# v of pair 0 through the casting queue first, and the attention steps of batch 1 moved: what it does to a fused attention and MoE kernel

## The chip, the cores and the metric

One core of one Trainium2 chip. The metric is the device time of one execution in microseconds (us), median of several. The time before is 287.01 us (three runs, 286.96 to 287.21). The profile's span, from the first to the last instruction, is some 2 us shorter than that time.

## The reference, cut to what matters

```python
def _attn_ref(q, k, v, g_norm):            # q, k, v: 8 batches, 8 heads, 576 rows, 64 columns, float32
    kv = np.einsum('bhsd,bhse->bhde', k, v)
    out = np.einsum('bhsd,bhde->bhse', q, kv)
    rms = np.sqrt(np.mean(out * out, axis=-1, keepdims=True) + 1e-06)
    return out / rms * g_norm

def _moe_ref(x, w_in, w_out):              # x: 4608 x 512, w_in: 512 x 2048, w_out: 2048 x 512
    h = x @ w_in
    g = h * (1.0 / (1.0 + np.exp(-1.702 * h)))
    return g @ w_out
```

The attention's result, reordered to 4608 rows of 512, is the x of the second part. Inputs and output are float32.

Of the kernel before, what the change touches and what calls it, by code (L numbers as in the profile page):

```python
# [12 lines left out]
P = 128  # L13
# [3 lines left out]
def kernel(  # L17
# [10 lines left out]
    nc = tc.nc  # L28
# [6 lines left out]
    KO = DM // P  # L35
# [8 lines left out]
    PE_ = 96  # L44
# [29 lines left out]
    vbuf = const.tile([P, NPAIR, 2 * NJ * D], F16)  # L74
# [5 lines left out]
    w_in_sb = const.tile([P, KO, DFF], F16)  # L80
# [6 lines left out]
    def early_src(n, b, c0, c1):  # L87
        return srcs[n][b, 2 * c0 : 2 * c1].rearrange("h (p j) d -> p h (j d)", j=NJ)

    def early_load(n, b, c0, c1):  # L90
        nc.gpsimd.dma_start(  # L91
            out=raw[n][0:PE_, c0:c1, :].rearrange("p c (l x) -> p (c l) x", l=2),
            in_=early_src(n, b, c0, c1),
        )
# [45 lines left out]


    first = {}
    for n in "kqv":
        first[n] = stage.tile([P, H, J * D], F32, name=f"{n}f", tag=f"{n}f")
        first[n] = first[n].rearrange("p h x -> p (h x)")[0:PE_, 0 : 2 * NJ * D]
        dst, src = first[n].rearrange("p (h x) -> p h x", h=2), early_src(n, 0, 0, 1)
        nc.sync.dma_start(out=dst, in_=src)
    g_row = const.tile([1, D], F32)
    nc.scalar.dma_start(out=g_row, in_=g_norm.unsqueeze(0))
    nc.vector.memset(ident, 0.0)  # L150
    nc.vector.memset(kvb[1], 0.0)
    nc.gpsimd.affine_select(
        out=ident,
        in_=ident,
# [6 lines left out]
    nc.gpsimd.memset(ones2, 0.0)  # L161
    nc.gpsimd.memset(ones2[0:D, 0:D], 1.0)
    nc.gpsimd.memset(ones2[D:P, D:P], 1.0)

    def load_w_in(f0, f1, k0=0, k1=KO):
        nc.gpsimd.dma_start(
            out=w_in_sb[:, k0:k1, f0 * P : f1 * P],
            in_=moe_w_in[k0 * P : k1 * P, f0 * P : f1 * P].rearrange(
                "(ko ki) f -> ki ko f", ki=P
            ),  # L170
        )

    for c in range(1, NPAIR):
        for n in "qkv":
            early_load(n, 0, c, c + 1)
    load_w_in(0, 4, 0, 2)
    load_w_in(0, 4, 2, KO)
    load_w_in(4, GROUP)
    load_w_in(GROUP, 10)
    load_w_in(10, FO)  # L180
# [264 lines left out]
    def dense(t, units1, units2, group, deep, hid=None):  # L445
# [21 lines left out]
        def project(mo, fo):  # L467
# [10 lines left out]
            if fo == FO - 1:  # L478
# [3 lines left out]
                if t == B:  # L482
                    store_rest(mo, 0, DM)
                elif t in HALVED and mo % 2:
                    store(t, mo - 1, mo + 1)

        def store_rest(mo, n0, n1):
            for g in range(2):
                rows = out[(2 * mo + g) * S : (2 * mo + g + 1) * S, n0:n1]
                if 2 * mo + g < EARLY:  # L490
                    p0 = SM % PE_
                    rows = rows[bass.DynSlice(NJ * p0 + SM // PE_, R, step=NJ), :]
                else:
                    rows = rows[SM:S, :]
                queue = (nc.sync, nc.scalar)[g]
                queue.dma_start(out=rows, in_=osb[g * R : (g + 1) * R, mo, n0:n1])
# [29 lines left out]
        if t < EARLY:  # L526

            n = 0
            while n < SM:
# [6 lines left out]
                n += m  # L536
        elif t < B and t not in HALVED:
            store(t, 0, J)

    def store(t, j0, j1):  # L540
        nc.sync.dma_start(
            out=out[t * S : t * S + SM, :].rearrange("(p j) m -> p j m", j=J)[:, j0:j1],
            in_=osbs[t][:, j0:j1],
        )
# [3 lines left out]

    nc.scalar.copy(qraw[0:PE_, 0, :], first["q"])
    nc.vector.tensor_copy(kraw[0:PE_, 0, :], first["k"])  # L550
    nc.vector.tensor_copy(vbuf[0:PE_, 0, :], first["v"])


    idle_ps = ps_h.tile([P, SM], F32, name="idle", tag="hT")
# [73 lines left out]
    nc.gpsimd.dma_start(out=g_all, in_=g_norm.unsqueeze(0).to_broadcast([P, D]))  # L628

    osbs = {}  # L630
    HALVED = (2, 3, 4, 5, 6)
    live = {0: a0}

    def start(b):
# [2 lines left out]
    for t in range(NT):  # L637
        b = t + 1
        u1, u2 = {}, {}

        def at1(i, f, *args):
            u1.setdefault(i, []).append(lambda: f(*args))

        def at2(i, f, *args):
            u2.setdefault(i, []).append(lambda: f(*args))

        def of(b, name, *args):
            return lambda: getattr(live[b], name)(*args)

        if t == 0:  # L650
            at1(7, of(0, "out", NPAIR))
            at2(4, setattr, a0, "ss_pool", Attention.ss_pool)
            at2(4, of(0, "ss", NPAIR, True))
            at2(4, of(0, "apply", NPAIR))
            at1(8, start, 1)
            for l in range(2):
                r = slice(l * PH, (l + 1) * PH)
                at1(8, nc.vector.memset, kpad[r, :, :, (1 - l) * D : (2 - l) * D], 0.0)
            for c in range(NPAIR):
                at1(12, of(1, "pack_q", c))  # L660
                at2(9 + 3 * c, of(1, "q", c))
                at2((21, 21, 33, 33)[c], of(1, "pack_k", c))
                at2((25, 27, 42, 43)[c], of(1, "kv", c))
                o = (31, 34, 50, 53)[c]
                at2(o, of(1, "out", c))
                if c == NPAIR - 1:
                    at2(46, load_kv, 2)
                at2((38, 46, 56, 59)[c], of(1, "ss", c))
                at2((38, 46, 56, 59)[c], of(1, "apply", c))
        elif b < B:  # L670
            if t == 1:
                at2(46, setattr, live[1], "ss_pool", Attention.ss_pool)
                at2(46, of(1, "out", NPAIR))
                at2(53, of(1, "ss", NPAIR))
                at2(53, of(1, "apply", NPAIR))
            f0 = 5 if t == 1 else 2
            at1(f0, cast_q, b)
            at1(f0, start, b)
            at1(f0, of(b, "transpose_q"))
            if t + 2 < B:  # L680
                at1(f0, load_q, t + 2)
                at1((10 if t == 1 else 9) + 4, load_kv, t + 2)
            for c in range(NPAIR):
                at1(f0, of(b, "pack_k", c))
                at1((10 if t == 1 else 9) + c, of(b, "kv", c))
            at2(6, nc.scalar.preload_act_table_set, "natural_log_exp_and_others")
            for j in range(J):
                at2((1, 4, 8, 11)[j], of(b, "rows", j))
            at2(7, of(b, "turn", 0))
            at2(16, of(b, "turn", 2))  # L690
            at2(27, of(b, "out", NPAIR))
            at2(36, of(b, "ss", NPAIR))
            at2(36, of(b, "apply", NPAIR))
        dense(t, u1, u2, (GROUP, 5)[t] if t < 2 else 0, t == 0, None if t else d0)
# [30 lines left out]
```

## The kernel before: the parts that the change touches

The kernel works batch by batch. While TensorE does the dense layers of batch t, the attention of batch t+1 is slipped in between. Only batch 0 has nothing to hide behind: its q, k and v, four pairs of heads, must be loaded first. Filler matmuls (`busy`) are there to keep TensorE's clock up meanwhile.

There are two ways in. The SP queue loads float32, and VectorE or ScalarE casts afterwards. The queue of GpSimd casts to 16 bits on the way; this text calls it **the casting queue**. One load of one tensor of one pair reads 295 kB and, when cast, writes 147 kB (the profile calls that 144 KB).

```python
    def early_load(n, b, c0, c1):                       # the casting queue
        nc.gpsimd.dma_start(out=raw[n][0:PE_, c0:c1, :]..., in_=early_src(n, b, c0, c1))
    # [cut]
    for n in "kqv":                                     # pair 0: float32, SP queue
        # [cut: the stage tile]
        nc.sync.dma_start(out=dst, in_=src)
    # [cut: g_row on the ACT queue, two memsets on VectorE]
    nc.gpsimd.affine_select(out=ident, ...)
    nc.gpsimd.memset(ones2, 0.0)                        # and two more
    for c in range(1, NPAIR):                           # pairs 1 to 3: nine casting loads
        for n in "qkv":
            early_load(n, 0, c, c + 1)
    load_w_in(0, 4, 0, 2)                               # five loads of w_in behind them
    # [cut: four more]

    nc.scalar.copy(qraw[0:PE_, 0, :], first["q"])       # the casts of pair 0
    nc.vector.tensor_copy(kraw[0:PE_, 0, :], first["k"])
    nc.vector.tensor_copy(vbuf[0:PE_, 0, :], first["v"])

    busy(12)
    a0.q(0)                                             # transposes of q
    busy(2)
    a0.kv(0)                                            # k^T v of pair 0
    # [cut: busy(2), out(0), q(1), kv(1), sums(0), out(1)]
    a0.q(2)
    a0.rs(0)
    busy(1)
    a0.kv(2)
    # [cut: sums(1), apply(0), busy(1), out(2), rs(1)]
    a0.q(3)
    a0.kv(3)
    # [cut: sums(2), apply(1), out(3), rs(2), apply(2), busy(3), then the dense matmuls of batch 0]

    # batch 1, between the matmuls of batch 0's second dense layer (the numbers are places there)
                at2((25, 27, 42, 43)[c], of(1, "kv", c))
                o = (31, 34, 50, 53)[c]
                at2(o, of(1, "out", c))
```

## Time and profile before

| what | before | from |
|---|---|---|
| time, median | 287.01 us | timed runs |
| span of the profiled execution | 284.9 us | the page |
| TensorE busy | 279.1 us, 98% | the page, busy shares |
| kv of pair 3 starts | 12.90 us | timeline |
| first dense matmul | 14.55 us | timeline |

The busy shares of the page (engine, busy us, share of the span, instructions) and its DMA queues (q0 is the casting queue, q1 the SP queue; packets, MB written, share of 16 engines):

```profile
PE 279.1 (98%) x1717; PEld 135.1 (47%) x1717; DVE 118.9 (42%) x230; ACT 156.1 (55%) x273; POOL 57.1 (20%) x82
...
q0 software_dynamic: 14960, 15.58, 33.5%
q1 hardware_dynamic: 38688, 22.39, 30.2%
```

The reader is to see that TensorE is the bound for the whole and that DMA isn't, on average. An average hides the opening, where TensorE waits for loads; the prediction below takes it apart.

### The profile page before, as it was taken

Reading aid. Unit: us, or ns where it says so; the run is one execution under the profiler, and the core shown is the slowest. Engines: PE = TensorE matmul, PEld = TensorE weight load, DVE = VectorE, ACT = ScalarE, POOL = GpSimd, SP = SyncE. Lnnn points to the kernel's source line nnn. Section 1 sums busy time; section 2 is a strip of 40 time slices with the busy share of each in tenths; the row PEclk is TensorE's granted clock in tenths of the full one; section 3 lists DMA queues with packets and bytes.
Section 4 is the critical chain, followed back from the end, with each engine's and each line's share of the span. In section 5 each row is a group of like instructions: output and inputs, shape, how many; then the busy total and the mean of one; then the engine's idle time right before and its main releaser. Section 6 shows DMA issues by size and latency. Waiting matters only on the chain.

```text
span 284.9 us, 4354 instructions
## 1 busy us (share of the span) xinstructions
PE 279.1 (98%) x1717; PEld 135.1 (47%) x1717; DVE 118.9 (42%) x230; ACT 156.1 (55%) x273; POOL 57.1 (20%) x82
## 2 busy tenths in 40 slices
PE   8899999999999999999999999999999999999995
PEld 2444544455445544554455445544454444444443
DVE  2550666527661657157713852286327400110001
ACT  2697439766575646574458536763666365016400
POOL 8931461111211121112011401130002100000000
PEclk9999999999999999999999999999999999999999
DMA  8999999995589358953797279925401410012022
GB/s 176 200 207 204 205 249 239 242 268 105 122 165 254 60 147 161 242 90 69 224 208 138 38 216 200 184 39 184 83 2 37 120 66 0 0 69 81 0 74 74
DMA packets 54070, 38.76 MB, mean 136 GB/s; under 512 B 31219, under 2 KB 50931, under 8 KB 53923
## 3 DMA queue, kind: packets, MB, share of 16 engines
q0 software_dynamic: 14960, 15.58, 33.5%
q1 hardware_dynamic: 38688, 22.39, 30.2%
q10 hardware_dynamic: 402, 0.52, 0.5%
q8 instruction: 13, 0.21, 0.3%
q14 instruction: 7, 0.05, 0.1%
HBM read 36.73 MB, written 9.44 MB: 162 GB/s over the span
## 4 chain that ended last, share of the span: by engine, by line
PE 93%; POOL 2%; DMA 2%; DVE 1%; issue 0%
PE hT L434 44%; PE o L471 42%; PE kvp L223 3%; DMA vbuf<-in_v_dram 2%; PE outR L287 2%; PE oh L503 1%; POOL kraw L91 1%; PE ss L335 1%; POOL qraw L91 1%; DVE kpad L214 1%; PE outT L255 0%; POOL vbuf L91 0%; PE q L412 0%; PE outT L266 0%; PE idle L558 0%
## 5 line engine op out<-in xcount | busy, mean ns | idle before, releaser
L471 PE MATMUL o<-w_out_sb,gT 128*128 128x512 f16 x560 | 130.7, 379 | 0.0
L443 ACT ACTIVATE gT<-hT 128x512 f16<-128x512 f32 x144 | 84.5, 599 | 76.5 <-PE hT L434 76.4
L434 PE MATMUL hT<-xT,w_in_sb 128*128 128x512 f16 x512 | 116.2, 379 | 0.0
L434 PEld LDWEIGHTS <-w_in_sb 128*128 128x128 f16 x576 | 54.6, 98 | 62.3 <-DMA w_in_sb<-in_moe_w_in_dram 0.5
L471 PEld LDWEIGHTS <-gT 128*128 128x128 f16 x560 | 52.9, 98 | 56.2 <-issue 0.2
L481 DVE COPY osb<-o 128x512 f32<-128x512 f32 x20 | 13.8, 690 | 62.4 <-PE o L471 62.4
L319 POOL TENSOR_TENSOR x<-xr,g_all 128x512 f16<-128x512 f32 x12 | 15.2, 1270 | 71.2 <-DVE xr L312 47.2
L214 DVE COPY kpad<-kraw 64x576 f16<-64x576 f16 x56 | 25.0, 446 | 2.0 <-DMA kraw<-in_k_dram 0.7
L298 DVE TENSOR_REDUCE sum<-sq 128x8 f32<-128x512 f16 x24 | 15.8, 679 | 19.9 <-ACT sq L295 19.9
L236 DVE CAST kvb<-kvp 64x128 f16<-64x128 f32 x28 | 8.1, 288 | 36.5 <-PE kvp L223 36.4
L312 DVE TENSOR_TENSOR xr<-outR,sum 128x512 f32<-128x512 f32 x24 | 15.5, 686 | 11.1 <-ACT sum L309 11.1
L112 POOL DMA_DIRECT2D kraw<-in_k_dram x16 | 9.9, 624 | 48.8 <-DVE kpad L214 42.8
L112 POOL DMA_DIRECT2D vbuf<-in_v_dram x16 | 9.7, 608 | 33.9 <-PE kvp L223 29.3
L319 DVE TENSOR_TENSOR x<-xr,g_all 128x512 f16<-128x512 f32 x12 | 15.2, 1267 | 0.7
L295 ACT ACTIVATE sq<-outR 128x512 f16<-128x512 f32 x24 | 13.6, 591 | 2.0 <-PE outR L287 1.6
L223 PEld LDWEIGHTS <-kpad 128*128 128x128 f16 x252 | 11.0, 98 | 7.0 <-DVE kpad L214 0.9
L434 PE MATMUL hT<-x_rem,w_in_sb 128*128 128x512 f16 x64 | 14.0, 379 | 0.0
L275 ACT ACTIVATE sq<-outT 128x512 f16<-128x512 f32 (+1 forms) x16 | 7.7, 481 | 10.4 <-PE outT L255 9.0
L481 ACT COPY osb<-o 128x512 f32<-128x512 f32 x15 | 8.7, 581 | 6.3 <-DMA out_dram<-osb 6.3
L223 PE MATMUL kvp<-vbuf,kpad 128*128 128x64 f16 x252 | 11.9, 193 | 0.1
L308 ACT ACTIVATE sum<-sum,eps_t 128x16 f32<-128x16 f32 x12 | 3.7, 308 | 15.0 <-DVE sum L298 14.9
L337 ACT ACTIVATE ln<-ss,eps_t 128x512 f32<-128x512 f32 (+1 forms) x16 | 9.4, 586 | 4.3 <-PE ss L335 4.1
(62 smaller groups left out, 141.5 us busy)
## 6 DMA issues: line engine op xcount, KB each, us to landing
qf<-in_q_dram SPq DMA_DIRECT2D x5, 1024.0 KB, 9.0
out_dram<-osb SPq DMA_DIRECT2D x10, 512.0 KB, 2.9
kraw<-in_k_dram POOLq DMA_DIRECT2D x12, 288.0 KB, 6.9
vbuf<-in_v_dram POOLq DMA_DIRECT2D x12, 288.0 KB, 5.5
w_out_sb<-in_moe_w_out_dram POOLq DMA_DIRECT2D x3, 512.0 KB, 14.4
out_dram<-osb SPq DMA_DIRECT2D x6, 192.0 KB, 5.5
qf<-in_q_dram POOLq DMA_DIRECT2D x1, 1024.0 KB, 11.1
out_dram<-osb SPq DMA_DIRECT2D x1, 1024.0 KB, 3.8
```

The lines of the kernel that those rows point to most:

```text
L112: nc.gpsimd.dma_start(out=raw[n][l * PH : (l + 1) * PH, c0:c1, 0 : NH * D], in_=srcs[n][b].rearrange("(c l) (p j) d -> l p c (j d)", l=2, ...
L214: nc.vector.tensor_copy(out=kpad[r, c, :, l * D : (l + 1) * D], in_=kraw[r, c, 0 : NH * D].rearrange("p (j d) -> p j d", j=NH),)
L223: nc.tensor.matmul(self.kvp[:, c, :], kpad[:, c, j, :], vbuf[:, c, j * D : (j + 1) * D], start=(j == 0), stop=(j == NH - 1),)
L295: nc.scalar.activation(sq, t, AFT.Square)
L298: nc.vector.tensor_reduce(out=self.sum2[:, j % 2, :], in_=sq.rearrange("p (h d) -> p h d", h=H), op=ALU.add, axis=mybir.AxisListType.X,)
L312: nc.vector.tensor_mul(xr[:, i], self.o[j + i].rearrange("p (h d) -> p h d", h=H), s2[:, i, :].unsqueeze(2).to_broadcast([P, H, D]),)
L319: (nc.vector if i else nc.gpsimd).tensor_mul(self.x16[:, j + i, :].rearrange("p (h d) -> p h d", h=H), xr[:, i], g_all.unsqueeze(1).to_bro ...
L337: nc.scalar.activation(ln[:, 0:n], t[:, 0:n], AFT.Ln, bias=eps_t, scale=1.0 / D)
L434: nc.tensor.matmul(self.h[fo], w_in_sb[:, ko, fo * P : (fo + 1) * P], self.x[:, ko], start=(ko == 0), stop=(ko == KO - 1),)
L443: nc.scalar.activation(self.gT[:, fo, :], self.h[fo], AFT.Gelu_apprx_sigmoid)
L471: nc.tensor.matmul(os[mo], gT[:, fo, mo * P : (mo + 1) * P], w_out_sb[:, fo, :], start=(fo == 0), stop=(fo == FO - 1),)
L481: copy(osb[:, mo, :], os[mo])
```

## The change

The intent: v of pair 0 isn't needed before kv of pair 0, so it can take the casting queue, and if it is the first load there, that queue starts before ident and ones are made instead of after. k and q then have the SP queue to themselves, and VectorE loses a cast. The moved steps of batch 1 fit the later or earlier arrival of its loads, and tile 7 is stored in two halves.

```diff
     first = {}
-    for n in "kqv":
+    early_load("v", 0, 0, 1)
+    for n in "kq":
 [cut]
+    early_load("q", 0, 1, 2)
     nc.gpsimd.affine_select(
 [cut: ones2; load_w_in only moves up in the text]
     for c in range(1, NPAIR):
-        for n in "qkv":
+        for n in "qkv"[c == 1 :]:
             early_load(n, 0, c, c + 1)
 [cut]
-    nc.vector.tensor_copy(vbuf[0:PE_, 0, :], first["v"])
 [cut]
-    HALVED = (2, 3, 4, 5, 6)
+    HALVED = (2, 3, 4, 5, 6, 7)
 [cut]
-                at2((25, 27, 42, 43)[c], of(1, "kv", c))
-                o = (31, 34, 50, 53)[c]
+                at2((27, 28, 42, 43)[c], of(1, "kv", c))
+                o = (32, 35, 50, 53)[c]
```

More of the change, by code (lines that the diff above doesn't have):

```diff
@@ L151, with load_w_in @@
     nc.vector.memset(kvb[1], 0.0)
+    def load_w_in(f0, f1, k0=0, k1=KO):
+        nc.gpsimd.dma_start(
+            out=w_in_sb[:, k0:k1, f0 * P : f1 * P],
+            in_=moe_w_in[k0 * P : k1 * P, f0 * P : f1 * P].rearrange(
+                "(ko ki) f -> ki ko f", ki=P
+            ),
+        )
+    early_load("q", 0, 1, 2)
     nc.gpsimd.affine_select(
@@ L163 @@
     nc.gpsimd.memset(ones2[D:P, D:P], 1.0)
-    def load_w_in(f0, f1, k0=0, k1=KO):
-        nc.gpsimd.dma_start(
-            out=w_in_sb[:, k0:k1, f0 * P : f1 * P],
-            in_=moe_w_in[k0 * P : k1 * P, f0 * P : f1 * P].rearrange(
-                "(ko ki) f -> ki ko f", ki=P
-            ),
-        )
     for c in range(1, NPAIR):
-        for n in "qkv":
+        for n in "qkv"[c == 1 :]:
             early_load(n, 0, c, c + 1)
```

## The prediction

> **What bounds the kernel now.** I first read the busy shares of the page, then busy time by stretch, the waits, the chain and the timeline of the opening, and last the DMA view in short windows. The page gives TensorE 279.1 us busy of a span of 284.9. The busy time by stretch (columns: stretch, PE, PEld, DVE, ACT, POOL, granted clock, DMA share, GB/s) says where the missing 5.8 us lie:
>
> ```profile
> 0.00:1.27 1.27, 0.00 (x0) 0.00 (x0) 0.39 (x4) 0.00 (x0) 0.46 (x6) 1.00 0.00 0
> 1.27:14.55 13.28, 12.30 (x128) 5.55 (x129) 5.48 (x13) 7.01 (x11) 12.46 (x21) 1.00 1.16 207
> 14.55:46.00 31.45, 31.36 (x200) 15.04 (x199) 13.58 (x28) 20.59 (x35) 12.14 (x19) 1.00 1.22 220
> 46.00:226.00 180.00, 180.00 (x1120) 88.60 (x1119) 94.27 (x177) 108.36 (x195) 32.05 (x38) 1.00 0.68 147
> 281.50:284.90 3.40, 0.00 (x0) 0.00 (x0) 0.29 (x1) 0.00 (x0) 0.00 (x0) 1.00 0.29 77
> ```
>
> From 46 us to the last matmul TensorE has no hole, at full clock: nothing outside it can shorten that. Of the rest, 1.27 us is start-up, 3.40 the last copy and store. Only 13.28 - 12.30 = 0.98 us in the opening and 31.45 - 31.36 = 0.09 up to 46 us are waits. So the change can win **1.07 us at most**, 0.4% of 287.01, unless it removes matmuls, and the two matmul streams have the same number of them.
>
> What the 0.98 us waits for, from the timeline of the opening (start, length, engine, line, operation; in brackets the idle time and what ended it):
>
> ```profile
> 1.79 0.82 POOL L91 DMA_DIRECT2D qraw<-in_q_dram  x1
> 5.28 0.83 ACT L549 CAST qraw<-qf 96x768 f16<-96x768 f32 x1 [2.69 <-DMA qf<-in_q_dram]
> 6.16 0.45 PE L389 MATMUL q<-ident,qraw 96*64 96x96 f16 x12
> 6.55 0.56 DVE L551 CAST vbuf<-vf 96x768 f16<-96x768 f32 x1 [1.68 <-DMA vf<-in_v_dram]
> 12.90 0.38 PE L372 MATMUL kv<-vbuf,kraw 96*64 96x64 f16 x12 [0.70 <-DMA vbuf<-in_v_dram]
> 16.51 4.86 PEld L434 LDWEIGHTS <-w_in_sb 128*128 128x128 f16 x24 [0.35 <-DMA w_in_sb<-in_moe_w_in_dram]
> 23.41 4.98 PEld L434 LDWEIGHTS <-w_in_sb 128*128 128x128 f16 x24 [0.20 <-DMA w_in_sb<-in_moe_w_in_dram]
> ```
>
> The one large hole is 0.70 us before kv of pair 3, whose v is the ninth and last attention load of GpSimd's queue. The last two lines matter as much: the weight loads that come behind it in that queue land just when TensorE wants them (0.35 and 0.20 us of weight-load wait, no matmul hole). TensorE and the casting queue run **neck and neck**. TensorE can't keep a gain bigger than the queue's own advance by more than a tenth or two.
>
> The chain of waits tells how that queue works:
>
> ```profile
> 1.85 0.77 POOL qraw L91
> 6.35 0.88 POOL kraw L91
> 7.23 5.54 DMA vbuf<-in_v_dram
> 12.90 0.40 PE kv L372 x12
> ```
>
> The last load is issued at 7.23 and lands 5.54 us later, a backlog. In the DMA view by window, packets of this queue first come at about 5.0 us, 3.2 after the first issue, and then run without a break at some 200 GB/s of written bytes. For 5.7 to 12.7 us (queue, packets, MB, share of engines) it reads:
>
> ```profile
> q0 software_dynamic: 1913, 1.40, 130.2%
> q1 hardware_dynamic: 3, 0.00, 0.2%
> ```
>
> 1.40 MB in 7.0 us is 0.2 MB per us, so a load of 144 KB (147 kB) costs 0.74 us. Nine from 5.0 end at 11.7, and a landing comes about 1 us after the last packet: 12.7, as seen (12.77). The SP queue's three float32 loads fill the engines from 1.8 to about 5.4 us.
>
> **What the Trainium skill says.** "DMA: Bandwidth & Descriptors", section "Issuing engines are not separate DMA queues": transfers of all issuing engines run on the same 16 DMA engines and interleave. The trace agrees: between 5.1 and 5.4 us the two queues moved 36 packets each. So v of pair 0 doesn't become free by changing queue. The same page, section "SWDGE vs HWDGE vs iDMA", says that a cast in flight is for GpSimd's descriptors alone, hence the queue; its "Latency and other measured facts" puts the first byte at 0.6 us from SP and about 1 us from GpSimd. Here SP's packets come 1.1 us after issue; GpSimd's took 3.2 us in the opening, and in the steady part (issue at 82.64, first packets after 83.8, full rate from about 85.0) 1.2 and 2.4 us. For full rate I use the measured 2.4 to 3.2.
>
> **The change part by part.**
> (1) v of pair 0 leaves the SP queue: 295 kB of float32 that shared engines with k and q go, and the 0.56 us cast on VectorE goes with them. Nothing waited for that cast: TensorE was doing filler matmuls until 7.16. Gain on the path: 0.
> (2) It becomes the first load on GpSimd, ahead of the ident and ones work, with q of pair 1 next. SP's first issue is at 0.75, so I put this one there: 1.79 - 0.75 = 1.04 us earlier. The queue carries ten attention loads instead of nine, +0.74. Net advance 1.04 - 0.74 = **0.30 us** for everything behind, if the engines are free and the queue doesn't run dry.
> (3) It may run dry once. The two early issues take 0.82 + 0.63, then ident and ones take 1.85 - 1.02 = 0.83, so k of pair 1 is issued near 3.03 instead of 2.61. With 2.4 to 3.2 us to full rate it flows from 5.4 to 6.2; before, it flowed from 5.0 + 0.74 + sharing, near 6.0. So the advance from there lies between +0.5 and -0.2.
> (4) k and q of pair 0 now meet v's packets from 3.2 to 4.0 us on. q's landing was 5.2 us, its cast ended 6.11, and TensorE took it at 6.16, right as the 12 fillers ended. Any delay of q shifts the opening; some 70 to 200 kB shared by halves makes it an estimated 0.2 to 0.5 us. It eats into the 0.70 us hole, not the end time at once: the hole leaves 0.2 to 0.5 us to win.
> (5) The kv steps of batch 1 move from 25 and 27 to 27 and 28, out from 31 and 34 to 32 and 35. These are the same matmuls in another order; the weight-load wait on kpad is 0.9 us in two times, but the matmul hole in all of that stretch is 0.09. Gain 0 to 0.09.
> (6) The store of tile 7 in two halves: it is issued near 254 us, the DMA share there is 0.13, and the end is the store after 281.5. Gain 0.
>
> Sum: the smaller of the hole left (0.2 to 0.5) and the queue's advance (centre 0.2, plus 0.1 of slack), plus up to 0.09. I take 0.3 us: 287.01 - 0.3 = **286.7**.
>
> **The rivals.**
> A: q is late by much more. If v and q of pair 1 reach full rate by 2.5 us, half the traffic is theirs while q waits; q lands 1 us later, q(0) starts near 7.2, and as its 6.05 us of serial work to the end of q(3) keep their length, kv of pair 3 comes at 13.2 instead of 12.9. Time 287.3. Against it: the slow ramp of GpSimd's queue.
> B: the queue runs dry and the weights land later. The w_in waits at 16.5 and 23.4 become matmul holes of about 0.2 us, time 287.2. For it: GpSimd's 0.63 us per issue is close to the 0.74 us per load.
> C: the full gain. Mixed traffic is denser (the SP queue alone fell to 259 packets in 3.3 to 4.8 us, 173 per us, while both together later made 240), so the engines finish the whole earlier, the 0.70 hole closes, the weights follow: 287.01 - 0.8 = 286.2.
> D: all hidden: 287.0.
>
> **Range and chances.** The ceiling of 1.07 us bounds it above, the rivals put it from 286.2 to 287.3, and the three runs of before spread by 0.25. A difference over 2% would need 5.7 us, which no part can bring: 0.005 each way.
>
> **What would show it.** Right: the stretch from 46 us on unchanged in busy time; v of pair 0 issued at about 0.75 us and k of pair 1 near 3.0; q's cast on ScalarE starting 5.4 to 5.8; the hole before kv of pair 3 under 0.5 us; the first dense matmul 0.2 to 0.5 us before 14.55; kpad weight-load waits shorter. Wrong: a filler-to-q(0) hole over 0.8 us (A), larger w_in waits (B), no hole at kv of pair 3 and the dense part over 0.6 us earlier (C). It would be wrong altogether if TensorE's clock or the tail changed.

## The result and the profile after

The changed kernel took **288.04 us** in the median of six runs, 287.34 to 289.51; the kernel before, run between them, 287.00 (286.87 to 287.51). The ratio is 1.0039, with a 95% interval of 1.0014 to 1.0063. A ratio here is the mean time of one kernel's fast runs over that of the other's fast runs of the same rounds, so it isn't quite the ratio of the medians quoted. The change costs some 1.1 us (0.0039 times 287), where 0.3 us of gain were forecast, and the time scatters over 2.2 us instead of 0.6.

The profiled execution was the fastest of the six (span 285.6). Its busy time by stretch, in the columns of before:

```profile
1.27:14.55 13.28, 10.96 (x126) 4.99 (x127) 4.49 (x12) 6.38 (x10) 12.75 (x22) 1.00 1.14 180
14.55:46.00 31.45, 31.39 (x200) 15.18 (x199) 13.94 (x29) 20.61 (x36) 12.52 (x20) 1.00 1.22 221
46.00:226.00 180.00, 180.00 (x1120) 88.43 (x1118) 94.32 (x177) 108.91 (x196) 32.08 (x38) 1.00 0.68 146
...
282.20:285.60 3.40, 0.00 (x0) 0.00 (x0) 0.28 (x1) 0.00 (x0) 0.00 (x0) 1.00 0.29 77
```

From 46 us on nothing changed, and the tail is 3.40 us again. The opening is where the time went: 10.96 us of matmuls instead of 12.30, and the DMA moved 180 GB/s instead of 207. (Not all of the missing matmul time is waiting: TensorE's clock came up to full at 4.2 us in this execution and at 5.7 in that of before, so the same fillers took 4.20 us instead of 4.92.)

The timeline of the opening, with the lines that answer to those shown of before:

```profile
1.31 0.82 POOL L91 DMA_DIRECT2D vbuf<-in_v_dram  x1 [0.86 <-POOLq L709]
2.13 0.64 POOL L91 DMA_DIRECT2D qraw<-in_q_dram  x1
...
3.64 0.65 POOL L91 DMA_DIRECT2D kraw<-in_k_dram  x1
...
5.24 0.83 ACT L550 CAST qraw<-qf 96x768 f16<-96x768 f32 x1 [2.66 <-DMA qf<-in_q_dram]
...
11.27 0.38 PE L373 MATMUL kv<-vbuf,kraw 96*64 96x64 f16 x12 [0.68 <-DMA vbuf<-in_v_dram]
...
13.53 0.38 PE L373 MATMUL kv<-vbuf,kraw 96*64 96x64 f16 x12 [0.72 <-DMA vbuf<-in_v_dram]
...
15.38 0.33 PEld L435 LDWEIGHTS <-w_in_sb 128*128 128x128 f16 x3 [0.55 <-DMA w_in_sb<-in_moe_w_in_dram]
```

q's cast on ScalarE starts at 5.24 us, as before (5.28): k and q were not delayed. But v of pair 0 was issued at 1.31 us, not at 0.75; k of pair 1 at 3.64 (before: 2.61); there are two holes for loads now, before kv of pair 2 and of pair 3; and kv of pair 3 starts 13.53 - 12.90 = 0.63 us later. The span is 285.57 - 284.93 = 0.64 us longer. That one number, **the start of kv of pair 3**, turned out to carry the end: in sixteen of the twenty traces the span ends 272.0 to 272.4 us after it, whatever was done to the loads (the four others, e2, r2, e6 and e9, are told below). In thirteen of the twenty, the two compared here among them, TensorE waits there for v of pair 3, the last of the attention's loads. In the seven others (e5, e6, e8, e9, e11, e12, r2) no wait stands before it, and an earlier late load, more fillers or a lower clock has set it.

Next, how fast the casting queue ran. For each of two kernels, the DMA view from 5 to 11 us, the line of the casting queue; before:

```profile
q0 software_dynamic: 1597, 1.14, 124.5%
```

and after:

```profile
q0 software_dynamic: 1505, 1.07, 124.3%
```

The queue of before began at 5.05 us and moved more in these 6 us than that of after, which had been running since 3.57. The trace keeps each packet's duration, which the views don't show, so I read it there. In the kernel before every 768-byte casting packet between 5.0 and 11.5 us took at most 79 ns. In the changed kernel the median is 79 ns too, but packets of 0.2 to 1.0 us are strewn in from 5.4 to 14.2 us. Below, **a stalled packet** is one of the casting queue that took over 160 ns and began before 11 us: none of them before, 24 after. That is no theory yet; it says where the bandwidth went.

Two more figures from the packet records. One load is 192 packets of 768 bytes, so the ends of the 192nd and of the last such packet give the queue's **pace** from its first load on: before, (12.46 - 6.12) / 8 = 0.79 us per load; after, (13.06 - 4.95) / 9 = 0.90. And the queue never ran dry: from its first packet to 13 us the time without one in flight comes to under 0.02 us in both. From 5.5 to 11.5 us there were 20.9 of its packets in flight on average before and 19.9 after, but 1.8 of the latter were stalled ones. That leaves 18.1 that moved, 13% fewer, which is the size of the loss of pace (an estimate).

### The profile page after: what moved, and what is told of

The parts are those of the page before. It is cut to its first block, busy times and chain, and to the rows that moved or that the text cites. A ratio compares the mean times of both kernels' runs of the same rounds, so it can differ in the third digit from the quotient of the medians.

```text
span 285.6 us, 4353 instructions
## 1 busy us (share of the span) xinstructions
PE 278.5 (98%) x1717; PEld 134.8 (47%) x1717; DVE 118.3 (41%) x229; ACT 156.1 (55%) x273; POOL 57.6 (20%) x83
## 4 chain that ended last, share of the span: by engine, by line
PE 93%; POOL 2%; DMA 2%; issue 0%; DVE 0%; POOLq 0%
PE hT L435 44%; PE o L472 42%; PE kvp L224 3%; DMA w_in_sb<-in_moe_w_in_dram 2%; PE outR L288 2%; PE oh L504 1%; POOL vbuf L91 1%; PE ss L336 1%; POOL qraw L91 1%; POOL kraw L91 1%; PE q L413 0%; PE outT L267 0%; PE outT L256 0%; POOL ident L162 0%; DVE osb L512 0%
## 5 line engine op out<-in xcount | busy, mean ns | idle before, releaser
L299 DVE TENSOR_REDUCE sum<-sq 128x8 f32<-128x512 f16 x24 | 15.8, 678 | 19.9 <-ACT sq L296 19.9
```

Source lines behind the costliest of these rows:

```text
L299: nc.vector.tensor_reduce(out=self.sum2[:, j % 2, :], in_=sq.rearrange("p (h d) -> p h d", h=H), op=ALU.add, axis=mybir.AxisListType.X,)
```

## The experiments

Eighteen kernels ran beside the kernel before. The diffs are against the kernel before unless said otherwise. This table comes from the traces (times in us) and the timed runs; "issued" counts the casting loads whose issue had ended when the first casting packet moved.

| run | loads on SP + cast | first issue | first packet | issued | stalled packets | kv of pair 3 | span less that | ratio to before (95%) |
|---|---|---|---|---|---|---|---|---|
| before | 3 + 9 | 1.79 | 5.05 | 4 | 0 | 12.90 | 272.0 | |
| r1_before_again | 3 + 9 | 1.79 | 4.81 | 4 | 0 | 13.00 | 272.0 | 1.0009 (0.9994 to 1.0024) |
| r3_before_third | 3 + 9 | 1.79 | 4.79 | 4 | 2 | 13.32 | 272.0 | one run |
| e1_steps_only | 3 + 9 | 1.79 | 4.14 | 3 | 18 | 13.41 | 272.4 | 1.0002 (0.9989 to 1.0015) |
| e13_before_held | 3 + 9 | 2.48 | 5.09 | 3 | 1 | 12.84 | 272.2 | 1.0007 (0.9990 to 1.0023) |
| e10_q_on_act | 2, 1 on ACT + 9 | 1.79 | 4.81 | 4 | 1 | 12.81 | 272.4 | 1.0003 (0.9984 to 1.0023) |
| e3_q_early_only | 3 + 9 | 1.30 | 3.62 | 1 | 21 | 13.23 | 272.0 | 1.0017 (1.0003 to 1.0031) |
| e5_four_on_sp | 4 + 8 | 1.79 | 4.37 | 3 | 13 | 13.83 | 272.2 | 1.0044 (1.0026 to 1.0061) |
| after | 2 + 10 | 1.31 | 3.57 | 2 | 24 | 13.53 | 272.0 | 1.0039 (1.0014 to 1.0063) |
| r2_after_again | 2 + 10 | 1.31 | 3.52 | 2 | 41 | 14.17 | 273.5 | 1.0043 (1.0027 to 1.0060) |
| e2_loads_only | 2 + 10 | 1.33 | 3.74 | 2 | 41 | 14.13 | 272.9 | 1.0047 (1.0033 to 1.0061) |
| e11_after_fillers | 2 + 10 | 1.33 | 3.61 | 2 | 39 | 14.09 | 272.1 | 1.0022 (1.0007 to 1.0037) |
| e4_v_cast_late | 2 + 10 | 1.79 | 3.67 | 2 | 48 | 13.84 | 272.1 | 1.0020 (1.0006 to 1.0033) |
| e15_third_sp_dummy | 3 + 10 | 1.79 | 4.82 | 4 | 0 | 13.52 | 272.0 | 1.0019 (0.9999 to 1.0039) |
| e16_after_dummy | 3 + 10 | 1.31 | 3.77 | 2 | 40 | 14.82 | 272.4 | 1.0077 (1.0057 to 1.0097) |
| e14_v_dropped | 2 + 9 | 1.79 | 3.90 | 3 | 41 | 13.16 | 272.3 | 1.0015 (0.9995 to 1.0035) |
| e8_all_cast | 0 + 12 | 1.80 | 3.32 | 2 | 55 | 15.10 | 272.4 | 1.0079 (1.0063 to 1.0095) |
| e9_cast_held | 2 + 10 | 3.01 | 4.55 | 1 | 51 | 15.15 | 273.2 | 1.0070 (1.0042 to 1.0098) |
| e12_held_longer | 2 + 10 | 4.50 | 6.03 | 2 | 57 | 16.82 | 272.1 | 1.0141 (1.0121 to 1.0161) |
| e6_after_merged | 2 + 7 | 1.33 | 3.87 | 2 | 57 | 17.35 | 273.4 | 1.0174 (1.0153 to 1.0194) |

A single trace of a kernel is one draw of its scatter; the ratios are the means. In e6, e8, e9, e12 and r2 the clock was at half for 3.4 to 10.2 us of the traced opening, so their times hold more than the loads. The pace goes with the stalls: 0.77 to 0.84 us per load in the six traces with at most two stalled packets, 0.86 to 1.06 in the fourteen others.

### First question: which part of the change costs the time?

My first theories: **A**, the tenth load of the casting queue costs 0.74 us and the earlier start gives back only 1.79 - 1.31 = 0.48; **B**, an early start itself makes packets stall. A rival to both: the moved steps.

**e1_steps_only**

```diff
-    HALVED = (2, 3, 4, 5, 6)
+    HALVED = (2, 3, 4, 5, 6, 7)
-                at2((25, 27, 42, 43)[c], of(1, "kv", c))
-                o = (31, 34, 50, 53)[c]
+                at2((27, 28, 42, 43)[c], of(1, "kv", c))
+                o = (32, 35, 50, 53)[c]
```

> The kernel before with only the moved kv and out steps of batch 1 and the halved store of tile 7. Every theory that puts the loss in the loads expects 287.0 us, within 0.2. If the moved steps cost the time, 287.6 or more.

Measured: 287.37 us against 287.21, ratio 1.0002. The steps and the halved store cost or win nothing that the noise (0.3 to 0.4 us) lets one see. Its opening is that of the kernel before, yet this trace has 18 stalled packets: the kernel before has them too, in some executions.

**e2_loads_only** (against the changed kernel)

```diff
-    HALVED = (2, 3, 4, 5, 6, 7)
+    HALVED = (2, 3, 4, 5, 6)
-                at2((27, 28, 42, 43)[c], of(1, "kv", c))
-                o = (32, 35, 50, 53)[c]
+                at2((25, 27, 42, 43)[c], of(1, "kv", c))
+                o = (31, 34, 50, 53)[c]
```

> The changed kernel with the steps and the store of tile 7 put back: the loads alone. Theories of the loads expect 287.8 to 288.4 us, as the changed kernel; the theory that the steps cost it expects 287.0.

Measured: 288.45, ratio 1.0047. The loads alone cost all of it. Its trace ends 272.9 us after kv of pair 3, not 272.0, in part since a w_in load came late as well (a matmul hole of 0.36 us at 18.25).

**e3_q_early_only**

```diff
+    early_load("q", 0, 1, 2)
     nc.gpsimd.affine_select(
 [cut]
-        for n in "qkv":
+        for n in "qkv"[c == 1 :]:
```

> v of pair 0 stays on the SP queue; only the cast load of q of pair 1 goes ahead of ident and ones, so the casting queue starts at 1.31 instead of 1.79 us with nine loads. Theory A (the tenth load outweighs the earlier start, 0.74 against 0.48 us) expects up to 0.48 us less than before: 286.6 to 287.0, casting packets steady at 79 ns. Theory B (an early start makes casting packets stall, some up to 975 ns) expects stalled packets between 5 and 14 us and 287.4 or more.

Measured: 287.68, ratio 1.0017, with 21 stalled packets. Theory A alone wanted a gain of up to 0.48 us. Issuing earlier, with no load added, doesn't help: it costs 0.5 us (0.0017 times 287), and the interval excludes no change, but only just. Its 21 stalled packets are hardly more than the 18 of e1, whose loads are unchanged.

**e4_v_cast_late** (against the changed kernel)

```diff
-    early_load("v", 0, 0, 1)
     for n in "kq":
 [cut]
-    early_load("q", 0, 1, 2)
     nc.gpsimd.affine_select(
 [cut]
+    early_load("v", 0, 0, 1)
     for c in range(1, NPAIR):
-        for n in "qkv"[c == 1 :]:
+        for n in "qkv":
```

> v of pair 0 as the first load of the casting queue, but behind ident and ones as q of pair 1 was before: ten loads, first issue at 1.79 us. Theory A expects the queue 0.74 us later than before: 287.6 to 287.9, worse by 0.5 than the changed kernel's share of A. Theory B expects no stalled packets as the start isn't early; its time is then also 287.6 to 287.9, but with less scatter than the changed kernel (within 0.5 us).

Measured: 287.74, ratio 1.0020, in the expected band and with little scatter (287.47 to 288.21), but not for A's reason alone: there are 48 stalled packets, which B hadn't expected as the first issue is at 1.79 again. So an early issue isn't the only way to get stalls.

### Second question: are the traces lucky draws, and is it the queue or the bytes?

**r1_before_again**: the kernel before, unchanged.

> The kernel before once more, for a second trace on the chip of the other three. Ratio 1.000. Read it for the casting queue: if its steady read rate (some 395 GB/s read, 200 written, from 5 to 14 us) belongs to the order of its loads, this trace shows it again, with the last w_in load landing 261.5 us before the end; if the first trace was a lucky one, the rate is as low (340) as in the changed kernel.

Measured: ratio 1.0009, no stalled packets, kv of pair 3 at 13.00. The clean queue is no lucky draw of one trace, although e1 shows that it isn't certain.

**r2_after_again**: the changed kernel, unchanged.

> The changed kernel once more, on the same chip: ratio 1.003 to 1.005. If the low rate from 5 to 14 us belongs to its loads, it is there again (some 3.05 MB read in these 9 us against 3.5), and the end is again 261.5 us behind the last w_in landing.

Measured: 288.38, ratio 1.0043, 41 stalled packets, 3.02 MB read from 5 to 14 us (before: 3.54). The profiled execution was its slowest, 289.47 us, and shows a second loss that the first trace didn't have. The busy time by stretch, columns as before (the seventh figure after the stretch and its length is the granted clock):

```profile
7.88:11.29 3.41, 2.20 (x40) 1.20 (x39) 0.90 (x3) 1.58 (x3) 3.04 (x6) 1.00 1.14 168
11.29:14.70 3.41, 3.01 (x41) 1.62 (x40) 1.54 (x4) 2.30 (x5) 2.15 (x3) 0.50 1.23 185
14.70:18.12 3.42, 3.42 (x9) 1.09 (x10) 1.78 (x4) 1.90 (x4) 2.75 (x4) 0.50 1.33 203
```

I cut the stretches where the trace's own record has the clock change. In 3.41 us TensorE had only 2.20 us of matmuls, because one hole had grown to 1.14 us:

```profile
9.57 0.38 PE L373 MATMUL kv<-vbuf,kraw 96*64 96x64 f16 x12 [1.14 <-DMA vbuf<-in_v_dram]
```

Thereupon the granted clock was 0.50 for 6.8 us. The span ends 273.5 us after kv of pair 3 instead of 272.0: 1.5 us lost on top of the late loads.

How often? Each run's record has its mean granted clock, and one window of 3.41 us at half costs 0.006 of it. Among the 16 timed executions with these loads it is under 0.995 in three: 0.988 and 0.994 in two of r2's four, 0.994 in one of e2's six. In the six executions of the result it is 0.998 to 1.0, also in the slowest (289.51 us, 0.998). So the clock is an occasional second loss and no part of the result's 1.1 us.

**e5_four_on_sp**: the change turned round.

```diff
+    first["q1"] = [cut: a second float32 tile]
+    nc.sync.dma_start(out=first["q1"]..., in_=early_src("q", 0, 1, 2))
 [cut]
-        for n in "qkv":
+        for n in "qkv"[c == 1 :]:
 [cut]
+    nc.scalar.copy(qraw[0:PE_, 1, :], first["q1"])
```

> The change turned round: v of pair 0 stays on the SP queue and q of pair 1 joins it there as float32 with a cast on ScalarE, so four loads on SP and eight on the casting queue, the same bytes read. Theory of the serial casting queue (each load in it costs 0.74 us of the path): 286.3 us, faster by 0.7. Theory of bytes (all loads read the same bytes on the same engines; only stalled packets of the casting queue, which come when that queue runs with a short backlog, make the difference): 287.0, within 0.4, few stalled packets since seven casts are queued when the SP loads end.

Measured: 288.03, ratio 1.0044. Both expectations fail: neither fewer casts nor equal bytes describe it. It has 13 stalled packets, and v of pair 0 lands later than before (its cast starts at 7.61 us instead of 6.55; kv of pair 0 waits 0.72 us for it).

**e6_after_merged** (against the changed kernel)

```diff
-    for c in range(1, NPAIR):
-        for n in "qkv"[c == 1 :]:
-            early_load(n, 0, c, c + 1)
+    for n in "kv":
+        early_load(n, 0, 1, 2)
+    for n in "qkv":
+        early_load(n, 0, 2, 4)
```

> The changed kernel with pairs 2 and 3 in one load per tensor, so seven loads are issued instead of ten for the same bytes, and the backlog grows faster. If the short backlog behind the early start makes the packets stall, the read rate from 7 to 14 us comes back to some 395 GB/s and the last w_in load lands 0.5 us or more earlier than in the changed kernel, though the opening's matmuls wait longer for pair 2 (total 287.5 to 288.5). If not, the rate stays near 340 and the last w_in lands no earlier.

Measured: 291.93, ratio 1.0174, 57 stalled packets. All attention loads were issued by 7.2 us, a long backlog, and the stalls went on to 14.3. So a short backlog at the moment isn't what stalls a packet. (The excess beyond the loads is the clock again: 0.50 for 10.2 us, after 3.41 us with 2.08 us of matmuls. This is the likely reason for its 273.4.)

### Third question: overlap of the two queues, more queues, or the clock?

**e8_all_cast**

```diff
-    for n in "kqv":  [cut: the SP loads and the three casts of pair 0]
-    for c in range(1, NPAIR):
+    for c in range(NPAIR):
         for n in "qkv":
             early_load(n, 0, c, c + 1)
```

> All three loads of pair 0 through the casting queue (q, k, v, then the rest, behind ident and ones), none on SP: twelve casts, no overlap of two queues in the opening. Overlap theory (packets stall because the casting queue starts while the SP queue still reads, and the 16 engines get out of step): few stalled packets, 395 GB/s read from 5 to 14 us, total 287.5 to 288.3 since nothing is read before 4 us. If the casting queue stalls by itself when it starts early, the rate is near 340 and the total 289 or more.

Measured: 289.39, ratio 1.0079, 55 stalled packets with nothing on SP at all.

**e9_cast_held** (against e4)

```diff
+    held = const.tile([P, 1280], F16)
+    nc.gpsimd.memset(held, 0.0)
     early_load("v", 0, 0, 1)
```

> The changed kernel with the casting queue held back: v of pair 0 as its first load, issued near 3 us behind a filler memset on GpSimd (the memset's tile is not used), so k and q have been read by the SP queue before the first cast packet. Overlap theory: few stalled packets, 395 GB/s from 5.5 us, the last w_in load lands no later than with the issue at 1.79 us (24.5) although the start is 1.2 us later; total 287.3 to 287.9. Without it each us of delay counts: 288.7 or more.

Measured: 289.49, ratio 1.0070, 51 stalled packets, although k and q had been read before the first casting packet. e8 and e9 together do away with the theory that the stalls need an overlap of the queues. (Its clock fell to 0.50 as well, hence 273.2.)

**e10_q_on_act**

```diff
-        nc.sync.dma_start(out=dst, in_=src)
+        (nc.scalar if n == "q" else nc.sync).dma_start(out=dst, in_=src)
```

> The kernel before with q of pair 0 on the ACT queue beside k and v on SP. If the SP phase is slow (230 to 260 GB/s from 3.3 to 5 us) because one queue can't keep the engines busy, two queues read more by 5 us (over 0.9 MB instead of 0.78) and the end comes up to 0.4 us earlier, 286.6. If it is slow for another cause, same as before, 287.0; if more queues mean more stalls, 287.5 or more.

Measured: 287.33 against 287.14, ratio 1.0003. It read as much by 5 us as the kernel before (0.78 MB each; 0.29 of it through the ACT queue), then ran clean, and kv of pair 3 starts at 12.81. A third queue bought nothing here. The Trainium skill says so: "DMA: Bandwidth & Descriptors", section "Rules for kernel authors", that spreading DMAs over SP, ACT and GpSimd for bandwidth doesn't help. This run agrees.

**e11_after_fillers** (against the changed kernel)

```diff
     a0.rs(0)
-    busy(1)
+    busy(4)
     a0.kv(2)
 [cut]
     a0.q(3)
+    busy(3)
     a0.kv(3)
```

> The changed kernel with three more filler matmuls ahead of kv of pair 2 and of pair 3, where it has holes of 0.7 us. Theory: in some executions the granted clock of TensorE falls to half for 6.8 us after a stretch of 3.4 us with only 2.2 us of matmuls; fillers keep it up, so executions of over 289 us vanish while the loads still cost their 0.8 us: median 287.8, scatter under 0.8 us, granted clock 0.998 to 1.0 in the trace. If only the loads count: median 288.2, scatter as before.

Measured: 287.86, ratio 1.0022; the four runs lie between 287.69 and 287.98. The median and the small scatter are as the theory of the clock expects, and the granted clock is 0.998 to 1.0 in all four. But this doesn't show that fillers won anything: with the clock down in three of 16 executions without them, none in four isn't rare; the result's own six executions had no fall and a ratio of 1.0039; and the intervals overlap. Its trace has 39 stalled packets and kv of pair 3 at 14.09, no better than the changed kernel. What made the ratio smaller stays open.

### Fourth question: what keeps the kernel before clean?

Every clean trace up to here had its first casting packet at 4.8 us or later. It might be a matter of time.

**e12_held_longer** (against e9)

```diff
-    held = const.tile([P, 1280], F16)
+    held = const.tile([P, 3072], F16)
```

> The changed kernel with the casting queue held to a first issue near 4.6 us, first packet near 6 us (the filler memset's tile is unused). If stalls come only when the queue starts before some 4.7 us: none here, 395 GB/s from 6.5 us. If they come with the changed set of loads however late the queue starts: 60 stalled packets or more, rate near 300 in the first 4 us of the queue. Total in either case over 289.5 us.

Measured: 290.98, first packet at 6.03, 57 stalled packets. It isn't a matter of time.

**e13_before_held**

```diff
+    held = const.tile([P, 640], F16)
+    nc.gpsimd.memset(held, 0.0)
     for c in range(1, NPAIR):
         for n in "qkv":
```

> The kernel before with its casting queue held back by some 0.6 us (first issue near 2.4, a filler memset on an unused tile). If a start after 4.8 us is what keeps the queue clean: few stalled packets, 395 GB/s, total 286.8 to 287.1 with less scatter than the kernel before. If each us of delay counts: 287.6.

Measured: 287.00 against 286.95, ratio 1.0007; one stalled packet. The first issue comes 0.69 us later and the time is the same: in the kernel before, the time of the first issue isn't what counts. The first packet came at 5.09, as in the trace of before (5.05).

**e14_v_dropped**

```diff
-    for n in "kqv":
+    for n in "kq":
 [cut]
-    nc.vector.tensor_copy(vbuf[0:PE_, 0, :], first["v"])
+    nc.vector.tensor_copy(vbuf[0:PE_, 0, :], first["k"])
```

> Wrong result on purpose: v of pair 0 is not loaded, its buffer is filled from k, so two loads on SP and nine on the casting queue, 0.295 MB less to read. Without stalls the last w_in load lands 0.75 us earlier than in the kernel before and the total is 286.3. If two SP loads alone bring the stalls, it reads no more by 22 us than the kernel before minus 0.2 MB at the same place in the order, and the total is 287.0 or more.

Measured: 287.36 against 286.95, ratio 1.0015 (two runs). **A load less, and not faster**: 41 stalled packets, kv of pair 3 at 13.16, where 12.90 - 0.74 = 12.2 was due if the missing load had moved all others forward (an estimate). The same nine casts as before got through the first load 0.96 us earlier (5.16 instead of 6.12) and through the last 0.25 us later (12.71 instead of 12.46). Its DMA view from 5 to 11 us, the casting queue's line:

```profile
q0 software_dynamic: 1466, 1.04, 123.5%
```

**r3_before_third**: the kernel before, one look.

> The kernel before a third time, one look: first casting packet at 4.8 us or later and few stalls if the clean start belongs to its order of loads; an earlier start should come with stalls, as in the run of the moved steps alone.

Measured: 287.1, first packet at 4.79, two stalled packets.

**e15_third_sp_dummy** (against e4: v of pair 0 is loaded on SP as well, and nobody reads it)

```diff
-    for n in "kq":
+    for n in "kqv":
```

> Ten casts from 1.79 us as in the run with the cast behind ident and ones (48 stalled packets before 11 us, v of pair 3 landed at 13.71), with v of pair 0 also loaded on SP as float32 and not used: 0.295 MB more to read. If the third SP load keeps the casting queue clean: under 5 stalled packets, first casting packet at 4.8 us, and v of pair 3 lands 0.74 us behind the kernel before, at 13.6, though more is read; total 287.7. If not: 30 or more stalled packets and a landing of 14.4, total 288.4.

Measured: 287.48 against 286.88, ratio 1.0019 (two runs). Its casting queue from 5 to 11 us:

```profile
q0 software_dynamic: 1609, 1.15, 125.5%
```

and that of e4, which differs by the useless load alone:

```profile
q0 software_dynamic: 1393, 0.99, 119.6%
```

0 stalled packets instead of 48, and kv of pair 3 at 13.52 instead of 13.84, with 0.295 MB more to read. The third SP load keeps the casting queue clean. In the time this wins nothing (1.0019 against e4's 1.0020): the clean queue just pays for the useless load. The tenth cast still costs: 13.52 against 12.90 to 13.32 in the three traces of the kernel before, and 0.5 us (0.0019 times 287) in the time, with an interval that just reaches zero.

**e16_after_dummy** (against the changed kernel)

```diff
-    for n in "kq":
+    for n in "kqv":
```

> The changed kernel with v of pair 0 also loaded on SP and not used. If the third SP load alone decides: few stalled packets, total 287.5 or less with the queue's early start kept. If the early issue of two casts stalls the queue by itself, as it did with nine casts (21 stalled packets): 20 or more, total 288.3 or more.

Measured: 289.14, ratio 1.0077, 40 stalled packets. With the two early issues the third SP load doesn't help. The profile shows how the stalls reach TensorE; the waits of TensorE in this kernel (waited for, us in total, times, longest) are

```profile
PE kv L373 <- DMA vbuf<-in_v_dram: 2.6, 4, 1.1
...
PE q L390 <- ACT qraw L550: 0.7, 1, 0.7
```

**What the runs leave.** Two parts of the change go with stalls, each alone: taking the third load off SP (e14 and e4 dirty, e15 clean) and issuing ahead of ident and ones (e16 dirty, 40, although SP has three loads; e15, without the early issues, 0). Each rests on one trace per kernel, and e3 adds little to the second, as e1 shows. In the table the six clean traces have four casting loads issued when the first packet moves (once three, e13), the fourteen with 13 and more stalled packets have one to three. That is a correlation. As an issue takes about 0.63 us, the number mostly restates how long the first packet came after the first issue (2.6 to 3.3 us in the clean traces, 1.5 to 2.6 in the others), and e1 has the very opening of before; it may be a sign and not the cause. **Why a packet stalls isn't settled**. A short backlog at the moment (e6), the overlap of the queues (e8, e9) and the time of the start (e12) are ruled out as the sole cause. The trace doesn't name the engine or the address of a packet, so it goes no further.

## Why the prediction was wrong

The prediction read the bound rightly: the opening alone can move, TensorE and the casting queue run neck and neck there, and the stretch from 46 us on and the tail stayed as they were. Point by point:

- **(1) Right in what it counted, wrong in leaving it there.** The cast on VectorE was off the path (in e1's trace kv of pair 0 waited 1.10 us for it, and kv of pair 3 still 0.58 for its own load). But the 295 kB taken off SP weren't neutral: e14 shows that dropping them, and nothing else, doesn't speed up the kernel, and its trace has 41 stalled packets.
- **(2) is the step that failed.** "Net advance 1.04 - 0.74 = 0.30 us". Its 1.04 was wrong as the time of the issue: I put GpSimd's first issue at 0.75 because SP's was there, and it was at 1.31 (1.30 to 1.33 in the five further kernels that issue ahead), 0.48 earlier than before. In the packets this did no harm: with one SP load less beside it the queue was through its first load at 4.95 instead of 6.12 us, 1.17 earlier. What failed is that each load behind was taken to cost what it did before (0.74 us by the prediction's window, 0.79 by these packets). At the old pace the last of ten loads would have ended near 4.95 + 9 * 0.79 = 12.1, some 0.4 us before the 12.46 of before, close to my 0.30. At the measured 0.90 it ended at 13.06, 0.60 after. Nine loads times 0.11 us are the 1.0 us between forecast and result. Both exceptions that I named, free engines and a queue that doesn't run dry, were thought of as idle time; the loss was in packets that took longer.
- **(3) had the right doubt and the wrong measure.** I let the queue lose 0.2 us at worst, by running dry. It didn't run dry and lost 1.0 us in the profiled execution; in r2 (pace 0.95, last packet at 13.59) it lost 1.4.
- **(4) did not happen.** q's cast started at 5.24 instead of 5.28 us: v's packets met only the end of q's. Rival A falls with it.
- **(5) and (6) were right in the sum.** The weight-load wait on kpad (24 to 46 us) fell from 0.9 us to 0.2, and e1, with these parts alone, has a ratio of 1.0002.
- **Rival B** had the direction and part of the picture (weights landing later: the first w_in load came at 15.34 us and was waited for, 0.55 us), with 287.2 us; its cause, a queue that runs dry, is refuted by the packets. Rival C counted on denser mixed traffic, which was indeed faster at first (0.90 MB read by 5 us instead of 0.78), and then slower (3.04 MB from 5 to 14 us instead of 3.54). D (no change) is outside the interval.
- **What none of the rivals had** is the clock. I wrote that the prediction would be wrong "altogether if TensorE's clock or the tail changed", and gave it no weight. In r2's execution it changed, and cost 1.5 us; in the result's own executions it didn't, so the forecast didn't fail by it. The Trainium skill names the mechanism ("TensorE: Matmul & The Clock Gate", section "What's actually happening": a window of some 3.4 us in which the engine idles brings the slow state). The spells at half clock in these traces last 3.41, 6.83 and 10.24 us, whole multiples of such a window, which agrees; but the window needn't be idle. In these traces a window of 3.41 us with 2.20 us of matmuls in it was enough, so the longest hole of 1.1 us was.

So the 1.1 us are late loads, as far as the traces show. In the profiled execution, the fastest, kv of pair 3 starts 0.63 us later and the span is 0.64 longer. In the other traces of these loads (r2, e2, e11) the last attention packet ends 1.1 to 1.2 us later than before (13.53 to 13.70 against 12.46), the size of the mean loss (e11's timed runs lost only 0.6 us, which its trace doesn't explain). That the stalled packets are what slows the pace is an estimate from the packets in flight, and no run takes the stalls away from the changed kernel and leaves all else: e15 is clean, but has a load more.

No run here beats the kernel before.

## What to carry to other kernels

When a load is moved between queues, don't only count its bytes and its place: look at how the receiving queue starts. Here a casting queue that had four loads issued before its first packet moved kept its pace, and the same queue started earlier, or with fewer issued, mostly lost more than the head start. This is a correlation to try first elsewhere, not a shown cause. And where TensorE waits for loads in its first 20 us, look up the granted clock by stretch: in r2 1.2 us of short holes in one window cost another 1.5. Fillers in front of the wait cost nothing visible in e11; that they help isn't shown.

## What the Trainium skill lacked or had wrong

- "DMA: Bandwidth & Descriptors" ("Latency and other measured facts") gives about 1 us to the first byte for GpSimd's DMAs. From the start of the issue, which itself takes 0.8 us, to the first packet it was 1.5 us with idle DMA engines (e8, e9, e12) and 1.9 to 3.3 us beside an SP queue (the other kernels).
- The same page doesn't say that one casting queue can run clean or with stalled packets depending on the order of the loads: 79 ns a packet when clean, single packets of up to 1.44 us otherwise (e4), and 0.77 to 0.84 us per load against 0.86 to 1.06.
- No page says that GpSimd's first DMA starts later than SP's when it is the engine's first work: 1.31 us against 0.75, while GpSimd's first compute instruction ran at 1.02 in the kernel before.
- "TensorE: Matmul & The Clock Gate" ("HAM oscillation — how this bites in real kernels") words the rule as no idle gaps over some 3.4 us; no page gives the matmul time that a window with several shorter gaps needs. Here the clock fell to half for 3.4 to 10.2 us after a window of 3.41 us with 0.70 to 2.20 us of matmuls and the longest hole of 1.1 us (r2), and held after windows with 2.24 (e8), 2.29 (e16), 2.30 (e11) and 2.40 us (the changed kernel).
